# Two layers of experts behind a scan: the blocks of empty rows move from ScalarE's queue to SyncE's

## The chip, the cores and the metric

One core of a Trainium2 chip runs the kernel. The metric is the device time of one execution in microseconds (us); the kernel before has a median of 1076.63 us in 3 runs (1074.83 to 1076.91).

## What is computed

A gated scan over 2 sequences of 5056 tokens with 256 channels gives 10112 rows. Two layers of 8 experts follow; in both, each row goes to one expert (the largest logit) and comes out weighted with that expert's gate:

```python
f = lower_bound + (1 - lower_bound) * sigmoid(f_logit)
h = f[:, t] * h + (1 - f[:, t]) * x[:, t]        # y[:, t] = h
for e in range(8):                               # layer 1, then layer 2 on its output
    mask = expert_idx == e
    out[mask] = gate_w[mask, None] * (relu(x[mask] @ w1[e]) @ w2[e])   # 256 -> 1024 -> 256
```

Layer 1 finds its logits from normalised rows and normalised expert vectors divided by tau, layer 2 from `x @ w_gate`.

## The kernel before

Rows are sorted by expert through a table in DRAM, one per layer (X[0], X[1]; the trace shows both as X). Each expert has a region of its own in it, large enough for all rows. A row is written to its expert's next free place by an indirect DMA of GpSimd (p_put for layer 1, m_slot for layer 2), as two fp16 halves of its 256 values, its gate and its number.

The matmuls work on tiles of 128 rows of one expert. A tile is loaded by SyncE with a transposing DMA (t_load: xT<-X), its gates and row numbers with a small one (exr<-X); four buffers hold such tiles (XB). The hidden width of 1024 is done in two halves, and a **unit** is one tile and one half: 24 matmuls into hps (mm1, L827), an eviction by ScalarE (hT, L835) whose remainder VectorE takes (L188), and three units later 12 matmuls (mm2, L849). For layer 1's output ScalarE, VectorE and GpSimd then make the row for layer 2 (squares L872, scaled halves L887, logits, rank, place); for layer 2's output ScalarE scales it and GpSimd writes it out.

Which tile belongs to which expert is known only at run time. So now and then a **plan** is made (checkpoint): from the counters of rows per expert (RK) VectorE works out a table of expert and first row for the next tiles (tab), and the engines read its entries into registers. Layer 1 has four plans after 16, 32, 48 and 64 groups of 128 rows and a last one after all of them, layer 2 has one after 65 and a last one. Up to the last plan only full tiles are used. Behind the last plan each expert's region ends in a tile that is only partly filled; to make that safe, one block of 128 empty rows (zrow, 258 words of 4 bytes each, 132 KB a block) is written behind each expert's last row. That is pad_rows: `pads` holds, per expert, the place of the first free row, the engine loads the eight numbers into registers (L705) and issues one DMA per expert (L708). In the kernel before ScalarE does this, one block in each of the eight units behind the plan (`padn` is 1):

```python
for e in range(E):
    at(now[0] + 1 + e // cfg["padn"], 13, pad_rows, m, pads, e)
```

The order is written out by hand: `at(unit, priority, function)` puts each piece of work into a unit, and from unit 17 on the queues of TensorE, SyncE, GpSimd and ScalarE keep that order; VectorE's is chosen by a scheduler. Weights of layer 2 are loaded (ws, 512 KB, from ScalarE's queue), split into fp16 halves (W, ScalarE L397 and VectorE L188) and come in units between the others.

Dependencies through X are declared by hand. Row writes carry group Xw, blocks Xp, reads Xr. x_write frees a write from waits for Xw and Xr; a row write is freed from Xp too, a block is not, so each block waits for the block before it. x_read keeps the first `xcnt[key]` writes as dependencies of a tile's load; for a tile of the last plan these are all row writes and the eight blocks. do_loads puts loads up to six units ahead into SyncE's order, and stops at a tile whose writes have not all been put into the program yet.

Of the kernel before, what the change touches and what calls it, by code (L numbers as in the profile page):

```python
# [17 lines left out]
P = 128  # L18
D = 256
E = 8  # L20
# [97 lines left out]
 't0at': (-3, 40),  # L118
 'w1at': (16766, 49534),
 'w2at': (82048, 114816),  # L120
 'padn': 1,
 'xq': 'S'}


# [1 line left out]
def scan_moe_moe_kernel(ctx, tc, xf, emb, cst, tmp, w1a, w2a, w1b, w2b, out, seq, cfg=CFG):  # L126
# [5 lines left out]
    DUM = E * CAP  # L132
# [45 lines left out]
    X = [dr.tile([DUM + P, RW // 2], I32, name=f"X{m}") for m in range(2)]  # L178
# [5 lines left out]
    V, A, G, T, SP = nc.vector, nc.scalar, nc.gpsimd, nc.tensor, nc.sync  # L184

    def stt(eng, out, in0, s, in1, op0, op1, **kw):
        assert eng is V
        return eng.scalar_tensor_tensor(out=out, in0=in0, scalar=s, in1=in1, op0=op0, op1=op1, **kw)  # L188

    def ts(eng, out, in0, s1, s2, op0, op1=None):  # L190
        if op1 is None:
            return eng.tensor_scalar(out=out, in0=in0, scalar1=s1, scalar2=None, op0=op0)  # L192
        return eng.tensor_scalar(out=out, in0=in0, scalar1=s1, scalar2=s2, op0=op0, op1=op1)  # L193

    def tt(eng, out, in0, in1, op):
        return eng.tensor_tensor(out=out, in0=in0, in1=in1, op=op)  # L196

    xw = [[], []]  # L200
    pval = {}

    def ins_of(i):
        return getattr(i, "ins", i)

    def x_write(m, i, group="Xw"):
        i = ins_of(i)
        tc.declare_no_dep(i, group=f"Xw{m}", reason="disjoint rows")
        tc.declare_no_dep(i, group=f"Xr{m}", reason="disjoint rows")
        if group == "Xw" and pval:  # L210
            tc.declare_no_dep(i, group=f"Xp{m}", reason="disjoint rows")
        tc.add_to_no_dep_group(f"{group}{m}", i)
        xw[m].append(i)

    def x_read(m, i, key):
        i = ins_of(i)
        assert len(xw[m]) >= xcnt[key]
        keep = xw[m][:xcnt[key]]
        tc.declare_no_dep(i, group=f"Xw{m}", keep=keep, reason="ordered by hand")
        if (m, E - 1) in pval:  # L220
            tc.declare_no_dep(i, group=f"Xp{m}", keep=keep, reason="ordered by hand")
        tc.add_to_no_dep_group(f"Xr{m}", i)
        for w in keep:
            tc.add_manual_dep(i, w.name, mybir.DependencyInfo(mybir.DependencyClass.Sync, mybir.DependencyReason.DATA),
                              reason="rows of the tile table")
# [55 lines left out]
    zrow = [None]  # L281
# [59 lines left out]
    def setup_c(em, tau_t, trf, wgf):  # L341
        z = zero_rows()
        for m in range(2):
            x_write(m, G.dma_start(out=X[m][DUM:DUM + P, :], in_=z))
        V.memset(ones16, 1.0)
        V.memset(c64, 64.0)
        s0 = sm.tile([P, G4 + CT, E], F16, name="s0", tag="s0", bufs=1)
        for e in range(E):
            V.memset(s0[:, :, e:e + 1], float(CAPT * e))
        yield  # L350
        T.matmul(out=RK, lhsT=ones16, rhs=s0, start=True, stop=True, skip_group_check=True)
        V.tensor_copy(out=tri16, in_=trf)
        yield
        ts(V, tri16b, tri16, -1.0, 1.0, ALU.mult, ALU.add)
        yield
        V.tensor_copy(out=id16, in_=idt)
        yield
        ts(V, idn, idt, -1.0 / 64.0, None, ALU.mult)
        yield
        for m in range(2):  # L360
            G.memset(pt[m], 0.0)
        yield
        ts(V, wgh, wgf, 64.0, None, ALU.mult)
        yield
        stt(V, wgl, wgf, 64.0, wgh, ALU.mult, ALU.subtract)


    now = [0]
# [316 lines left out]
    def p_put(q, rows):  # L685
        p = pq[q]
        for i in rows:
            if i >= p["g"]:
                return
            x_write(0, G.indirect_dma_start(out=X[0], out_offset=IndirectOffsetOnAxis(ap=p["sl"][:, i, 0:1], axis=0),  # L690
                                            in_=p["row"][:, i, :].bitcast(I32), in_offset=None, bounds_check=BOUND,
                                            oob_is_err=False))
            yield
# [4 lines left out]
    nums = {}  # L698
    counted = [0, 0]

    preg = [A.alloc_register(f"pa{i}") for i in range(E)]

    def pad_rows(m, pads, e):
        if e == 0:
            A.load(preg, pads[0:1, 0:E])  # L705
            for i in range(E):
                pval[m, i] = A.snap(preg[i], donate=True, min_val=0, max_val=DUM)
        x_write(m, A.dma_start(out=X[m][ds(pval[m, e], P), :], in_=zrow[0]), "Xp")  # L708

    def checkpoint(m, n, final, key, done):  # L710
        c8 = RK[:, rkb[m][0]:rkb[m][0] + 1, :]
        if final:
            pads = tb.tile([P, E], I32, name="pads", tag=f"pads{m}")
            ts(V, pads, c8[:, 0, :], pid, None, ALU.add)
            for e in range(E):
                at(now[0] + 1 + e // cfg["padn"], 13, pad_rows, m, pads, e)
        xcnt[key] = 1 + done + (E if final else 0)
        assert counted[m] == done
        ct = tb.tile([P, 6, E], F32, name="ct", tag="ct")
        ci = tb.tile([P, E], I32, name="ci", tag="ci")  # L720
        stt(V, ci, c8[:, 0, :], float(P - 1 if final else 0), ebase, ALU.add, ALU.subtract)
        ts(V, ci, ci, 7, None, ALU.arith_shift_right)
        av, q, ex, v, w, tk = (ct[:, i] for i in range(6))
        V.tensor_copy(out=v, in_=ci)
        tt(V, av, v, pt[m], ALU.subtract)
        V.tensor_tensor_scan(out=q, data0=av, data1=av, initial=0.0, op0=ALU.add, op1=ALU.bypass)
        tt(V, ex, q, av, ALU.subtract)
        tt(V, v, pt[m], ex, ALU.subtract)
        stt(V, v, v, float(P), ebase, ALU.mult, ALU.add)
        tt(V, w[:, 0:E - 1], v[:, 1:E], v[:, 0:E - 1], ALU.subtract)  # L730
        ts(V, w[:, E - 1:E], v[:, E - 1:E], -1.0, float(DUM), ALU.mult, ALU.add)
        tab = tb.tile([P, 2, n], I32, name="tab", tag=f"tab{key}" if final or n > 4 else f"tab4_{int(key) % 8}")
        step = -(-n // -(-n // (D // (E + 1))))
        for j0 in range(0, n, step):
            k = min(step, n - j0)
            lew = op.tile([P, D], F32, name="le", tag="ob")
            le = lew[:, 0:k * E].rearrange("p (n e) -> p n e", e=E)
            ef = lew[:, k * E:k * (E + 1)].unsqueeze(2)
            ei, ri = (tab[:, i, j0:j0 + k] for i in range(2))
            jj = jt[:, j0:j0 + k]  # L740
            tt(V, le, q.unsqueeze(1).to_broadcast([P, k, E]), jj.unsqueeze(2).to_broadcast([P, k, E]), ALU.is_le)
            V.tensor_reduce(out=ef, in_=le, axis=AX.X, op=ALU.add)
            ts(V, ei, ef[:, :, 0], float(E - 1), float(ESTEP), ALU.min, ALU.mult)
            tt(V, le, le, w.unsqueeze(1).to_broadcast([P, k, E]), ALU.mult)
            V.tensor_reduce(out=ef, in_=le, axis=AX.X, op=ALU.add)
            stt(V, ef[:, :, 0], jj, float(P), ef[:, :, 0], ALU.mult, ALU.add)
            i = ts(V, ri, ef[:, :, 0], v[:, 0:1], float(DUM), ALU.add, ALU.min)
        if not final:
            ts(V, tk, ex, -1.0, float(n), ALU.mult, ALU.add)
            ts(V, tk, tk, 0.0, None, ALU.max)  # L750
            tt(V, tk, tk, av, ALU.min)
            tt(V, pt[m], pt[m], tk, ALU.add)
        if not tablast:
            tablast.append(ins_of(i))
        tabs[key] = tuple(tab[:, i] for i in range(2))
        if final:
            num = tb.tile([P, 1], I32, name="num", tag=f"num{m}")
            V.tensor_copy(out=num, in_=q[:, E - 1:E])
            nums[m] = num
# [311 lines left out]
    def at(s, prio, fn, *a):  # L1071
        seqn[0] += 1
        slots.setdefault(s, []).append((prio, seqn[0], fn, a))
# [154 lines left out]
    def cp1():  # L1228
        for m, cnt, n, fin, key in cpl:
            if m == 1 and key not in xcnt and cnt <= routed[0]:  # L1230
                checkpoint(m, n, fin, key, routed[0])
# [84 lines left out]
    with ExitStack() as region:  # L1316
# [5 lines left out]
        i = first - 2  # L1322
# [117 lines left out]
```

## Time and profile before

| | before |
|---|---|
| median of 3 runs | 1076.63 us (1074.83 to 1076.91) |
| profiled execution | 1075.63 us |
| its span, first to last instruction | 1073.8 us |
| TensorE busy | 1003.0 us (93%) |
| VectorE, ScalarE, GpSimd busy | 604.3, 525.3, 432.7 us |
| mean granted TensorE clock | 0.981 |
| bytes moved by DMA | 132.72 MB |

The profile gives, for one execution, the time each engine worked, and for each gap of an engine what ended it (the releaser). PE is TensorE, DVE VectorE, ACT ScalarE, POOL GpSimd, SP SyncE; ACTq and SPq are instructions that only issue a DMA or load registers. A clock of 1.00 is 2.4 GHz, one of 0.50 is 1.2 GHz. Times in us count from the first instruction.

### The profile page before, as it was taken

What the parts mean: (1) busy time and instruction counts of PE and PEld (TensorE: products, weight loads), DVE (VectorE), ACT (ScalarE), POOL (GpSimd) and SP (SyncE); (2) the same over time, 40 slices, a digit from 0 to 9 for tenths busy, and PEclk for the clock granted to TensorE, in tenths of its full rate; (3) what the DMA queues carried; (4) which work ended last, traced back from release to release, by engine and by line L of the source; (5) the groups of instructions that cost most, each with busy time, mean ns of one, the idle gap of its engine ahead of it and who ended that gap; (6) DMA issues with size and microseconds to landing.
All of it is one profiled execution on the core that took longest, in us unless ns stands there. A gap on an engine that the chain in (4) does not pass through costs nothing. (4 is left out here: it accounts for less than half of the span.)

```text
span 1073.8 us, 37047 instructions
## 1 busy us (share of the span) xinstructions
PE 1003.0 (93%) x13267; PEld 933.6 (87%) x13267; DVE 604.3 (56%) x2007; ACT 525.3 (49%) x1301; POOL 432.7 (40%) x864
## 2 busy tenths in 40 slices
PE   4557999999999999889999999899999999999997
PEld 4436889999999998779999998899999999999997
DVE  8989767787778776556429876543222222222221
ACT  6888455655555654456336564543333333333332
POOL 4276756667776665222101551143222222222222
PEclk9967999999999999989999999999999999999999
DMA  9699425876665773555459589843322222222220
GB/s 352 204 331 236 120 68 115 136 142 115 130 134 135 137 120 91 154 156 151 108 113 259 121 173 219 157 100 84 55 55 51 51 51 52 46 52 44 46 51 31
DMA packets 195616, 132.72 MB, mean 124 GB/s; under 512 B 169601, under 2 KB 172558, under 8 KB 195440
## 3 DMA queue, kind: packets, MB, share of 16 engines
q1 hardware_dynamic: 170080, 58.07, 27.5%
q10 hardware_dynamic: 13504, 40.74, 15.3%
q0 software_dynamic: 11856, 31.51, 11.0%
q8 instruction: 118, 1.93, 0.8%
q14 instruction: 58, 0.48, 0.2%
HBM read 58.89 MB, written 38.85 MB: 91 GB/s over the span
## 5 line engine op out<-in xcount | busy, mean ns | idle before, releaser
L827 PE MATMUL hps<-xT,W 128*128 128x128 f16 x7968 | 508.4, 220 | 16.7 <-DVE hT L188 5.8
L827 PEld LDWEIGHTS <-W 128*128 x7968 | 476.5, 98 | 29.5 <-issue 16.3
L849 PE MATMUL ops<-W,hT 128*128 x3984 | 492.5, 273 | 2.8 <-ACT W L397 1.0
L188 DVE SCALAR_TENSOR_TENSOR hT<-hps,hT 128x512 f16<-128x512 f32 x332 | 228.3, 688 | 343.3 <-ACT hT L835 325.9
L849 PEld LDWEIGHTS <-hT 128*128 128x128 f16 x3984 | 375.1, 98 | 44.1 <-issue 4.1
L835 ACT ACTIVATE hT<-hps 128x512 f16<-128x512 f32 x332 | 197.7, 596 | 336.9 <-PE hps L827 258.5
L1017 POOL DMA_INDIRECT out<-osum,ti x83 | 81.3, 979 | 301.2 <-ACT osum L1013 176.6
L995 POOL DMA_INDIRECT X<-trow,tsl x83 | 98.4, 1186 | 49.5 <-DVE tsl L188 16.4
L690 POOL DMA_INDIRECT X<-row,sl x79 | 88.8, 1124 | 69.8 <-issue 25.3
L1013 ACT ACTIVATE osum<-ops,exr 128x256 f32<-128x256 f32 x62 | 29.4, 474 | 47.0 <-PE ops L849 44.8
L196 POOL TENSOR_TENSOR lf<-exr,us 128x2 f32<-128x2 f32 (+1 forms) x42 | 9.5, 226 | 105.2 <-DVE us L192 52.0
L188 DVE SCALAR_TENSOR_TENSOR W<-ws,W 128x1024 f16<-128x1024 f32 x34 | 41.4, 1221 | 7.3 <-ACT W L397 7.2
L531 PE MATMUL yt<-cs,xf 128*128 128x128 f32 x126 | 27.9, 299 | 16.2 <-DVE xf L516 13.6
L516 DVE TENSOR_TENSOR_SCAN xf<-xf 128x256 f32<-128x256 f32 (+3 forms) x64 | 42.7, 708 | 0.1
L397 ACT ACTIVATE W<-ws 128x1024 f16<-128x1024 f32 x35 | 36.9, 1058 | 9.1 <-DMA ws<-w1b 5.0
L872 ACT ACTIVATE trow<-osum 128x256 f16<-128x256 f32 x83 | 35.1, 423 | 12.4 <-DMA X<-trow,tsl 4.9
L861 ACT ACTIVATE osum<-ops 128x256 f32<-128x256 f32 x58 | 22.2, 382 | 35.4 <-PE ops L849 29.0
L188 DVE SCALAR_TENSOR_TENSOR trow<-osum,tsc,trow 128x256 f16<-128x256 f32 x83 | 37.4, 481 | 3.3 <-ACT trow L887 1.7
L533 PEld LDWEIGHTS yt<-cs,xf 128*128 128x128 f32 x252 | 35.3, 204 | 0.8 <-issue 0.7
L188 DVE SCALAR_TENSOR_TENSOR row<-yt,sc,row 128x256 f16<-128x256 f32 x79 | 36.0, 472 | 0.0
L887 ACT ACTIVATE trow<-osum,tsc 128x256 f16<-128x256 f32 x62 | 28.1, 500 | 14.8 <-DVE tsc L193 11.9
L571 ACT ACTIVATE row<-yt,sc 128x256 f16<-128x256 f32 x79 | 33.1, 478 | 3.2 <-DVE sc L193 3.2
(161 smaller groups left out, 956.6 us busy)
## 6 DMA issues: line engine op xcount, KB each, us to landing
xf<-xf ACTq DMA_DIRECT2D x28, 512.0 KB
ws<-w1b ACTq DMA_DIRECT2D x16, 512.0 KB
ws<-w2b ACTq DMA_DIRECT2D x16, 512.0 KB
W<-w1a SPq DMA_DIRECT2D x11, 512.0 KB
W<-xf SPq DMA_DIRECT2D x8, 512.0 KB
ws<-w2a ACTq DMA_DIRECT2D x8, 512.0 KB
WD<-wq SPq DMA_DIRECT2D x8, 512.0 KB
W<-WD SPq DMA_DIRECT2D x8, 512.0 KB
```

Of the source, the lines that this page charges most:

```text
L188: return eng.scalar_tensor_tensor(out=out, in0=in0, scalar=s, in1=in1, op0=op0, op1=op1, **kw)
L397: A.activation(out=hi, in_=src, func=ACTF.Copy, scale=64.0)
L516: V.tensor_tensor_scan(out=t[:, k, lo:hi], data0=t[:, 2 + k, lo:hi], data1=t[:, k, lo:hi], initial=init, op0=ALU.mult, op1=ALU.subtract)
L533: T.matmul(out=yt[:, D:D + E], lhsT=t[:, k, i * P:(i + 1) * P], rhs=ide[:, (1 - k) * (P + E):(1 - k) * (P + E) + E], start=(k == 0), stop= ...
L571: A.activation(out=p["row"][:, o + i, 0:D], in_=yv(d["yt"][i]), func=ACTF.Copy, scale=p["sc"][:, o + i:o + i + 1])
L690: x_write(0, G.indirect_dma_start(out=X[0], out_offset=IndirectOffsetOnAxis(ap=p["sl"][:, i, 0:1], axis=0), in_=p["row"][:, i, :].bitcast( ...
L827: T.matmul(out=hps[:, c, :], lhsT=w, rhs=xt[:, a, :], start=(n == 0), stop=(n == 5))
L835: A.activation(out=hh[:, 0], in_=hps, func=ACTF.Relu)
L849: T.matmul(out=o, lhsT=hT[:, a + k, :], rhs=w[:, b * D:(b + 1) * D], start=(first and k == 0 and n == 0), stop=(last and k == 3 and n == 2))
L872: A.activation(out=d["row"][:, i, D:2 * D], in_=t["O"], func=ACTF.Square, scale=0.25, accum_out=d["ss"][:, i:i + 1])
L995: x_write(1, G.indirect_dma_start(out=X[1], out_offset=IndirectOffsetOnAxis(ap=sl[:, i, 0:1], axis=0), in_=d["row"][:, i].bitcast(I32), in ...
L1017: i = ins_of(G.indirect_dma_start(out=out, out_offset=IndirectOffsetOnAxis(ap=ti, axis=0), in_=r, in_offset=None, bounds_check=N - 1, oob_ ...
```

## The change

SyncE takes the place of ScalarE in pad_rows. The eight blocks of a layer are issued in one run, in the first unit behind the plan with priority 0, ahead of that unit's tile loads (do_loads has priority 1). And a block is freed from waits for other blocks: x_write declares no dependency on group Xp as soon as a block of the layer exists.

```diff
     xw = [[], []]
+    xpad = [[], []]
     pval = {}
...
-        if group == "Xw" and pval:
+        if xpad[m]:
             tc.declare_no_dep(i, group=f"Xp{m}", reason="disjoint rows")
         tc.add_to_no_dep_group(f"{group}{m}", i)
         xw[m].append(i)
+        if group == "Xp":
+            xpad[m].append(i)
...
-    preg = [A.alloc_register(f"pa{i}") for i in range(E)]
-
-    def pad_rows(m, pads, e):
-        if e == 0:
-            A.load(preg, pads[0:1, 0:E])
-            for i in range(E):
-                pval[m, i] = A.snap(preg[i], donate=True, min_val=0, max_val=DUM)
-        x_write(m, A.dma_start(out=X[m][ds(pval[m, e], P), :], in_=zrow[0]), "Xp")
+    preg = [SP.alloc_register(f"pa{i}") for i in range(E)]
+
+    pnil = SP.alloc_register("pnil")
+
+    def pad_rows(m, pads):
+        SP.load(preg, pads[0:1, 0:E])
+        for e in range(E):
+            SP.reg_mov(pnil, e)
+            pval[m, e] = SP.snap(preg[e], donate=True, min_val=0, max_val=DUM)
+            x_write(m, SP.dma_start(out=X[m][ds(pval[m, e], P), :], in_=zrow[0]), "Xp")
+        SP.reg_mov(pnil, E)
...
-            for e in range(E):
-                at(now[0] + 1 + e // cfg["padn"], 13, pad_rows, m, pads, e)
+            at(now[0] + 1, 0, pad_rows, m, pads)
```

In the order of instructions this looks as follows. The names in square brackets are what an instruction waits for: DMAHW0 to DMAHW7 are the completion counters that all DMAs of SyncE's and ScalarE's queues share in turn, DMASW those of GpSimd's, the others the engines. ISA rows are register work.

ScalarE behind layer 1's last plan, before: the eight blocks lie between evictions, squares and weight loads (two of the eight are shown), and the second one waits for a second counter, that of the block before it.

```order
L861 ACTIVATE osum<-ops 128x256 [waits PE_49]
L705 TENSOR_LOAD pads [waits DVE_49]
L708 ISA
L708 DMA X_99<-zrow 128x258 [waits DMAHW4_49]
L835 ACTIVATE hT<-hps 128x512 [waits PE_49]
...
L384 DMA ws<-w1b 128x1024
L708 ISA
L708 DMA X_99<-zrow 128x258 [waits DMAHW4_49,DMAHW0_49]
L872 ACTIVATE trow,tss<-osum 128x256 [waits DMASW5_49,DMASW4_49,Activation_49]
```

The same place now:

```order
L865 ACTIVATE osum<-ops 128x256 [waits PE_49]
L839 ACTIVATE hT<-hps 128x512 [waits PE_49]
...
L386 DMA ws<-w1b 128x1024 [waits DMAHW2_49]
L876 ACTIVATE trow,tss<-osum 128x256 [waits DMASW5_49,DMASW4_49,Activation_49]
```

The register load and the blocks are gone from ScalarE, and nothing else has changed its place there.

SyncE behind layer 1's last plan, before: two loads of tiles of the plan before, and then the first tile of the last plan, whose load waits for twelve counters.

```order
L802 DMA_TRANSPOSE xT<-X_99 128x4x128 [waits DMAHW2_49,PE_49]
L809 ISA
L809 DMA exr<-X_99 128x2 [waits DMAHW3_49]
L802 ISA
L802 DMA_TRANSPOSE xT<-X_99 128x4x128 [waits DMAHW5_49,PE_49]
L809 ISA
L809 DMA exr<-X_99 128x2 [waits DMAHW6_49,Pool_49]
L791 TENSOR_LOAD tab [waits DVE_49]
L802 ISA
L802 DMA_TRANSPOSE xT<-X_99 128x4x128 [waits DMAHW1_49,DMAHW2_49,DMAHW0_49,DMAHW3_49,DMASW7_49,DMAHW4_49,DMASW6_49,DMAHW6_49,DMASW3_49,DMAHW7_49,DMASW2_49,PE_49]
```

The same place now (six of the eight blocks left out):

```order
L708 TENSOR_LOAD pads [waits DVE_49]
L712 ISA
L712 DMA X_99<-zrow 128x258 [waits DMAHW2_49]
...
L712 DMA X_99<-zrow 128x258 [waits DMAHW1_49]
L806 ISA
L806 DMA_TRANSPOSE xT<-X_99 128x4x128 [waits DMAHW3_49,PE_49]
...
L806 DMA_TRANSPOSE xT<-X_99 128x4x128 [waits DMAHW5_49,PE_49]
...
L795 TENSOR_LOAD tab [waits DVE_49]
L806 ISA
L806 DMA_TRANSPOSE xT<-X_99 128x4x128 [waits DMAHW0_49,DMASW7_49,DMAHW1_49,DMASW6_49,DMAHW2_49,DMASW3_49,DMAHW7_49,DMASW2_49,PE_49]
```

The register load and eight blocks stand ahead of the two loads of the older plan; each block waits for one counter.

SyncE behind layer 2's last plan, now:

```order
L806 DMA_TRANSPOSE xT<-X_100 128x4x128 [waits DMAHW7_49,DMAHW0_49,PE_49]
L708 TENSOR_LOAD pads [waits DVE_49]
L712 ISA
L712 DMA X_100<-zrow 128x258 [waits DMAHW1_49]
...
L712 DMA X_100<-zrow 128x258 [waits DMAHW7_49]
L712 ISA
L712 DMA X_100<-zrow 128x258 [waits DMAHW0_49]
L712 ISA
L712 DMA X_100<-zrow 128x258 [waits DMAHW1_49]
L806 ISA
L806 DMA_TRANSPOSE xT<-X_100 128x4x128 [waits DMAHW3_49,PE_49]
```

Here the first load shown is layer 2's 17th and the last one its 18th; before, the 18th followed the 17th directly. The eighth block waits for the counter that the first block waited for.

## Rows read from the trace of the kernel before

**Rows 1.** Busy by stage: us, engines' busy us, PE clock, DMA share, GB/s

```profile
430.00:470.00 40.00, 32.13 (x409) 28.84 (x407) 18.67 (x71) 17.71 (x43) 10.29 (x20) 0.91 0.52 148
470.00:560.00 90.00, 89.63 (x1261) 84.92 (x1260) 46.11 (x147) 43.77 (x97) 14.65 (x32) 1.00 0.53 127
655.00:690.00 35.00, 29.44 (x387) 26.99 (x385) 19.36 (x31) 17.44 (x31) 0.18 (x1) 1.00 1.07 195
690.00:800.00 110.00, 110.00 (x1502) 104.39 (x1500) 37.91 (x63) 39.78 (x72) 36.49 (x62) 1.00 0.36 74
```

**Rows 2.** Instructions on pads and zrow: ns min/median/max, first and last start

```profile
L192 DVE TENSOR_SCALAR pads<-RK,cs x2: 226/226/226, 425.4 to 649.3; 128x8 int32<-128x8 f32 x2
L705 ACTq TENSOR_LOAD <-pads x2: 542/641/740, 426.4 to 655.9; - x2
...
L708 ACTq DMA_DIRECT2D X<-zrow x16: 338/338/391, 427.3 to 684.1; - x16
```

**Rows 3.** Waits of ScalarE, 425 to 460 us: total us, times, longest

```profile
ACT hT L835 <- DMA X<-zrow: 6.1, 3, 2.8
...
ACT trow L872 <- DMA X<-zrow: 3.4, 2, 2.3
```

**Rows 4.** Waits of SyncE's queue, 420 to 470 us

```profile
SPq L802 <- DMA X<-zrow: 24.1, 1, 24.1
```

**Rows 5.** Timeline of SyncE, layer 1: start, us, instruction

```profile
427.70 1.19 SPq L802 DMA_TRANSPOSE xT<-X  x1
...
458.39 1.21 SPq L802 DMA_TRANSPOSE xT<-X  x1
```

**Rows 6.** Waits of ScalarE, 645 to 690 us

```profile
ACT hT L835 <- DMA X<-zrow: 11.0, 6, 3.2
```

**Rows 7.** Groups of TensorE, 418 to 500 us: busy, mean ns | idle before, releasers

```profile
L915 PE MATMUL x2p<-id,trow 128*128 128x128 f16 x48 | 4.3, 220 | 2.7 <-ACT trow L887 1.5 <-DVE toh L188 0.6 <-PEq L1294 0.3
```

**Rows 8.** Timeline of TensorE, layer 1; in brackets idle time before, releaser

```profile
449.75 1.50 PE L827 MATMUL hps<-xT,W 128*128 128x128 f16 x24
...
452.40 1.50 PE L827 MATMUL hps<-xT,W 128*128 128x128 f16 x24
...
461.65 2.72 PE L827 MATMUL hps<-xT,W 128*128 128x128 f16 x24 [3.99 <-DMA xT<-X]
464.16 2.76 PE L849 MATMUL ops<-W,hT 128*128 x12
466.72 1.83 PE L827 MATMUL hps<-xT,W 128*128 128x128 f16 x24
...
471.29 1.47 PE L849 MATMUL ops<-W,hT 128*128 x12
```

**Rows 9.** Timeline of TensorE, layer 2

```profile
657.46 1.50 PE L827 MATMUL hps<-xT,W 128*128 128x128 f16 x24 [0.45 <-DMA xT<-X]
...
663.18 1.50 PE L827 MATMUL hps<-xT,W 128*128 128x128 f16 x24
...
669.98 1.50 PE L827 MATMUL hps<-xT,W 128*128 128x128 f16 x24 [1.34 <-DVE hT L188]
...
680.00 1.50 PE L827 MATMUL hps<-xT,W 128*128 128x128 f16 x24 [1.91 <-DVE hT L188]
...
683.40 1.50 PE L827 MATMUL hps<-xT,W 128*128 128x128 f16 x24 [0.59 <-DVE hT L188]
...
688.56 1.51 PE L849 MATMUL ops<-W,hT 128*128 x12 [1.01 <-ACT W L397]
```

**Rows 10.** Timeline of SyncE, layer 2

```profile
649.29 1.19 SPq L802 DMA_TRANSPOSE xT<-X  x1
...
653.42 1.19 SPq L802 DMA_TRANSPOSE xT<-X  x1
```

**Rows 11.** Timeline of ScalarE, layer 2

```profile
652.57 0.35 ACTq L384 DMA_DIRECT2D ws<-w2b  x1
...
659.78 1.06 ACT L397 ACTIVATE W<-ws 128x1024 f16<-128x1024 f32 x1 [2.15 <-DMA ws<-w2b]
```

More of the change, by code (lines that the diff above doesn't have):

```diff
@@ L120 @@
  'w2at': (82048, 114816),
- 'padn': 1,
  'xq': 'S'}
```

## The prediction

> **What bounds the kernel now.** I read the busy table by stage first. From 690 us on TensorE is busy for all of its 110 us, and between the two plans, in 470 to 560 us, for 89.63 of 90: it is the engine that sets the time. The reader is to look at the two stages in which it isn't full: in 430 to 470 us it is busy for 32.13 of 40 us at a mean granted clock of 0.91, and in 655 to 690 us for 29.44 of 35 us at full clock [rows 1]. These are the stretches behind the two plans: the first of ScalarE's blocks of empty rows is issued at 427.3 us, the last one at 684.1 us, eight per layer [rows 2]. Since TensorE is full behind each stretch, a microsecond won there should reach the end, and I count it one to one.
>
> Second, the waits. In the first stretch ScalarE waits 6.1 us ahead of evictions (hT) and 3.4 us ahead of squares (trow) for blocks to land [rows 3]. Squares and evictions themselves need nothing of the blocks; they only stand behind one on ScalarE's queue, and each block waits for the one before it. SyncE waits 24.1 us, in one piece, for the same blocks [rows 4]: between its load at 427.70 and the next one at 458.39 us [rows 5] it stands, because the first tile of the last plan may be read only when all eight blocks have landed, and ScalarE lets them out one per unit. In the second stretch ScalarE's evictions wait 11.0 us for blocks [rows 6].
>
> Third, what of this TensorE feels. First layer: 1.5 us ahead of a transposition for rows that ScalarE made late, and 0.6 us for a mask (toh) that VectorE makes from ScalarE's squares [rows 7]; then 3.99 us until the first tile of the last plan (xT) is there. Behind that gap the engine runs at the lower of its two clocks, 1.2 instead of 2.4 GHz, for three groups: 2.72 us where the same 24 matmuls take 1.50, 2.76 where the 12 take 1.47, and 1.83 for 1.50 [rows 8]. Second layer [rows 9]: 1.34, 1.91 and 0.59 us for hT, which VectorE could finish only after ScalarE's late eviction, and 1.01 us for a weight half (W) that ScalarE had still to copy.
>
> **The change, first layer.** Gaps of 0.6 + 1.5 + 3.99 = 6.09 us, and (2.72 - 1.50) + (2.76 - 1.47) + (1.83 - 1.50) = 2.84 us of slow clock: **8.93 us**, of which I take all as gone. What comes in its place on SyncE: it reads the counts two loads earlier in its order than its long wait, ahead of the load at 427.70 us and the one before that. VectorE wrote the counts at 425.4 us in 0.23 [rows 2], so SyncE stands until about 425.7 us, reads registers for 0.64 and issues eight DMAs of 0.34 us [rows 2]; with register work I allow 0.4 to 0.55 us each, 3.2 to 4.4 us, and it is through at 429.5 to 431 us. Queued behind are the two loads of the old plan. The tile loaded at 427.70 us is the last before the gap and feeds the groups of 449.75 and 452.40 us, its forerunner's two groups lie some 5 us before those [rows 5, 8]. The load whose landing the first layer shows took from 458.39 to 461.65 us, 3.26 us [rows 5, 8]; even at 8.17 us (the slowest seen, below) one issued at 431 us is there by 439, and needed near 444. So the block run is covered by about five microseconds; without that cover it would cost what the load is late. The first tile of the last plan can then be asked for as soon as a buffer is free, in the middle of the 430s, 20 us before its use. Next late after the 3.99 us is thus nothing on SyncE, and ScalarE and VectorE are busy for 17.71 and 18.67 of these 40 us [rows 1].
>
> **The change, second layer.** Gone are 1.34 + 1.91 + 0.59 = 3.84 us for hT and, with ScalarE no longer behind, the 1.01 us for the weights: **4.85 us**. But here SyncE has little cover. Each unit, about 2.65 us (449.75 to 452.40), takes a new tile, with four buffers, and the load that started at 649.29 us was waited for until 657.46, 8.17 us [rows 8 to 10]: transfers are slow there, beside weights of 512 KB, one of which, issued at 652.57 us, held ScalarE's copy up until 659.78 [rows 11]. The eight blocks now stand ahead of the load that started at 653.42 us [rows 10]. 0.64 for the registers and 3.2 to 4.4 for the blocks put it at 657.3 to 658.5 us. The seventh block also waits for a completion counter that may be that of the weights landing near 659.8 us; with that, the load starts near 660.9. Its tile was needed at 663.18 us, two groups after the one at 657.46 [rows 9]. Landing 3.26 us after its start, it is late by nothing to 1.0 us; at 8.17 us by up to 5.9, and a pause of that size may bring the slow clock, 2.84 us by the first layer's rows. Lower bound 0: an earlier load of another tile is no gain while TensorE is full. Upper bound 5.9 + 2.84 = 8.7 us. I take **2.0 us**: 1.0 by the quiet price, and about 1 more because the blocks on the queue ahead, 8 x 132 KB = 1.06 MB, need 5.4 us at this stage's 195 GB/s [rows 1], a little longer than their issue lasts.
>
> **What else moves.** ScalarE sheds 16 issues of 0.34 and two register loads of 0.64 us, 6.7 us in all [rows 2]; it is idle for half of both stretches, so I give that nothing. The same 16 transfers run, crowded into two bursts; near the first nothing is in need of the queue, the second is in the 2.0 us.
>
> The sum: -8.93 - 4.85 + 2.0 = **-11.78 us** against the profiled execution's 1075.63 us, 1063.85 us; the median is 1.0 us above that execution, so **1064.9 us**.
>
> **A rule against the change.** ScalarE lost 6.1 + 3.4 + 11.0 = 20.5 us to waits for the blocks and 16 x 0.34 = 5.4 us to issuing them [rows 2, 3, 6]. The Trainium skill, DMA: Bandwidth & Descriptors, section Issuing engines are not separate DMA queues, says that DMAs started from several engines run on the same 16 DMA engines and interleave, and that another issuing engine saves only the time to initiate them, usually small beside the transfer. By that alone the change would be worth about nothing (rival c); the rows speak against it, since most of the loss is order and waiting on the issuing queue.
>
> **The rivals.**
>
> (a) The burst only moves the loss to the tile loads of the second layer. For: the load of 8.17 us, and the 0.45 us that TensorE already waited for it [rows 9, 10]. Against: a block is a quarter of one weight load. It costs 8.7 instead of 2.0 us: -8.93 - 4.85 + 8.7 = -5.1, so 1071.5 us.
>
> (b) Slower: the eight blocks still land one after the other, now on SyncE, and hold up every tile load of the second layer. In the first layer they took from 427.3 until SyncE was released near 458.4 us, 31 us or 3.9 each; at that price the load of 653.42 us would start at 685 and land at 688, 25 us late: -13.78 + 25 = +11, so 1088 us. It decides the sign from a blockade of some 20 us on (13.8 us won and the 6 us that are covered), 2.5 us per block. Against: in the new order a block waits for one counter each, not for the block before; only the last may share its counter with the first.
>
> (c) Nothing changes: only issue time moves, ScalarE's waits lie beside other work, and the first tile of the last plan is held by the rows' other writers until then anyway. For: TensorE's gaps are small beside ScalarE's waits. Against: SyncE's one wait names the blocks. Price: at best the small gaps, up to 2 us, so 1074.6 to 1076.6 us.
>
> **How the numbers follow.** The forecast gets 0.69 (1061 to 1068 us), (a) 0.22, (b) 0.04, (c) 0.05. For the range I take the forecast and (a): downwards no loss in the second layer (1062.9) and, since nobody's wait explains 1.5 us of what 430 to 470 us still lacks (40 - 32.13 - 6.09 = 1.8), these gone too, 1061, rounded to 1060.5; upwards (a), rounded to 1072. About 0.2%, 2.2 us, is what a measurement of this kernel can tell from no change. Faster by more: 0.69 + 0.22 = 0.91; within: (c), 0.05; slower: (b), 0.04.
>
> **What would show it.** First layer: no wait of ScalarE for X<-zrow, SyncE's first load of the last plan near 435 instead of 458 us, no gap of several microseconds and clock 1.00 in 430 to 470 us. If ScalarE still keeps TensorE waiting there, my 2.1 us of small gaps are wrong; if SyncE does, the 6.83 us of gap and slow clock. Second layer: TensorE's gaps ahead of its groups now put down to xT, not to hT; their sum against my 2.0 us decides between the forecast and (a). If SyncE's own waits show block after block, it is (b). I am wrong altogether if both stretches gain and the same time comes back as gaps of TensorE between 470 and 640 us or behind 690 us.

## The result and the profile after

The changed kernel has a median of 1064.08 us in 10 runs (1062.0 to 1072.43), the kernel before 1075.81 us in 10 runs on the same chip (1071.8 to 1082.44). The ratio is 0.9902, with a 95% interval of 0.9873 to 0.9932: 10.5 us less, 7.3 to 13.7. Forecast was 1064.9 us. On a second chip the ratio was 0.9934 (0.9905 to 0.9962), 7.1 us. All ratios here are formed from single runs and not from the medians, and leave out three runs in a slower state (two of "layer 2 alone" and one of before, below), which medians and ranges count. So the sign was right; whether the mechanism and the terms were is the question of the experiments.

The profiled execution of after took 1063.67 us (span 1061.8, mean granted clock 0.984), 11.96 us less than that of before. Its stages, in the form of [rows 1]; the last two rows are as long as the stretches of before that begin when VectorE writes the counts and end at 470 and 690 us:

```profile
430.00:470.00 40.00, 39.48 (x572) 37.13 (x570) 26.30 (x91) 25.03 (x60) 13.04 (x28) 1.00 0.80 188
470.00:560.00 90.00, 88.81 (x1226) 83.49 (x1224) 45.17 (x133) 41.88 (x91) 11.52 (x24) 1.00 0.64 135
640.00:655.00 15.00, 9.58 (x126) 8.88 (x124) 8.99 (x20) 6.43 (x11) 0.00 (x0) 0.99 1.09 263
690.00:800.00 110.00, 110.00 (x1493) 104.30 (x1491) 35.66 (x58) 38.94 (x71) 34.07 (x58) 1.00 0.35 69
423.00:467.60 44.60, 44.08 (x638) 41.49 (x637) 30.81 (x121) 26.61 (x63) 16.40 (x29) 1.00 0.80 191
635.50:676.20 40.70, 35.04 (x459) 33.05 (x458) 24.27 (x50) 21.62 (x37) 1.65 (x2) 0.96 0.93 198
```

The same two stretches of before:

```profile
425.40:470.00 44.60, 36.73 (x476) 33.22 (x474) 23.11 (x98) 19.28 (x46) 13.78 (x25) 0.92 0.52 145
649.30:690.00 40.70, 35.14 (x465) 32.41 (x464) 24.94 (x51) 22.21 (x38) 1.08 (x2) 1.00 1.08 208
```

Behind the first plan TensorE is busy for 44.08 of 44.60 us instead of 36.73, at full clock. Behind the second it is busy for no longer than before (35.04 against 35.14 us), and at 0.96 instead of 1.00: in this pair of executions the second layer won nothing. The instructions on the counts and the blocks, against [rows 2], say the same by their times:

```profile
L191 DVE TENSOR_SCALAR pads<-RK,cs x2: 211/216/220, 423.0 to 635.5; 128x8 int32<-128x8 f32 x2
L708 SPq TENSOR_LOAD <-pads x2: 527/529/531, 423.3 to 639.0; - x2
...
L712 SPq DMA_DIRECT2D X<-zrow x16: 332/332/1227, 424.0 to 646.2; - x16
```

The first plan stands 2.4 us earlier (423.0 instead of 425.4), the second 13.8 us (635.5 instead of 649.3), the end 12.0. Ahead of the first plan both kernels run the same program, so its 2.4 us are not the change's. It brought 11.4 us between the plans, and behind the second it lost 1.8.

SyncE behind the first plan, against [rows 5] (start, us, instruction), and its one wait for blocks, against 24.1 us in [rows 4]:

```profile
423.99 4.53 SPq L712 DMA_DIRECT2D X<-zrow  x8
428.71 1.61 SPq L806 DMA_TRANSPOSE xT<-X  x1
...
431.14 1.20 SPq L806 DMA_TRANSPOSE xT<-X  x1
...
436.43 1.21 SPq L806 DMA_TRANSPOSE xT<-X  x1
```

```profile
SPq L806 <- DMA X<-zrow: 0.3, 1, 0.3
```

The eight blocks take 4.53 us, the two loads of the older plan follow at once, and the first tile of the last plan is asked for at 436.43 instead of 458.39 us. ScalarE's waits of [rows 3] have shrunk to one of 2.9 us (trow), which TensorE doesn't feel: between 418 and 475 us its only two gaps above 0.3 us are those below, against 3.99 us and three groups at the lower clock in [rows 8].

```profile
460.31 0.61 PE L919 MATMUL x2p<-id,trow 128*128 128x128 f16 x8 [0.52 <-DVE tse L981]
472.77 0.61 PE L919 MATMUL x2p<-id,trow 128*128 128x128 f16 x8 [0.95 <-PEq L1298]
```

SyncE and TensorE behind the second plan, against [rows 9, 10]:

```profile
639.68 6.81 SPq L712 DMA_DIRECT2D X<-zrow  x8
646.72 12.76 SPq L806 DMA_TRANSPOSE xT<-X  x5
```

```profile
655.24 2.72 PE L831 MATMUL hps<-xT,W 128*128 128x128 f16 x24 [5.66 <-DMA xT<-X]
657.75 1.69 PE L853 MATMUL ops<-W,hT 128*128 x12
```

The gaps for hT and W of [rows 9] are gone, and ScalarE waits for no block any more. In their place stands one gap for a tile. The run of blocks lasts 6.81 us; the load behind it begins at 646.72 us, its tile was needed at 655.24 - 5.66 = 649.58 and came at 655.24, 8.5 us after the issue. A load of the quiet price would have been 0.4 us late. Behind the gap TensorE again runs at the lower clock for a group and part of a second.

### The profile page after: what moved, and what is told of

It reads as the page before. It is cut to its first block, busy times and chain, and to the rows that moved or that the text cites. A ratio compares the mean times of both kernels' runs of the same rounds, so it can differ in the third digit from the quotient of the medians.

```text
span 1061.8 us, 37047 instructions
## 1 busy us (share of the span) xinstructions
PE 996.5 (94%) x13267; PEld 932.1 (88%) x13267; DVE 603.8 (57%) x2007; ACT 529.3 (50%) x1301; POOL 431.7 (41%) x864
## 5 line engine op out<-in xcount | busy, mean ns | idle before, releaser
L533 PE MATMUL yt<-cs,xf 128*128 128x128 f32 x126 | 28.2, 300 | 16.7 <-DVE xf L518 13.8
L891 ACT ACTIVATE trow<-osum,tsc 128x256 f16<-128x256 f32 x62 | 28.1, 500 | 16.0 <-DVE tsc L192 11.4
L187 DVE SCALAR_TENSOR_TENSOR xf<-xf 128x512 f32<-128x512 f32 (+1 forms) x32 | 21.8, 682 | 23.2 <-POOL xf L192 19.4
```

## The experiments

The theory: what was won is the order (all blocks early) and the blocks' independence of one another; in the second layer the run holds up tile loads, as the prediction's 2.0 us say. Its rivals: only ScalarE's queue matters; the blocks are bound to land one after another; or the loss of the second layer is larger than priced and can be avoided. All kernels but the repeat of after set per layer the engine, the first unit behind the plan, the units per block (0: all in one run) and the priority, in one table in place of after's fixed call. Of after the table would be:

```python
pads_at = (('SP', 1, 0, 0), ('SP', 1, 0, 0))    # layer 1, layer 2
```

and of before `('A', 1, 1, 13)` twice, chained, though the table's pad_rows then differs from before's in one dependency, told under "One layer at a time". `chained` below stands for the pair in x_write that says of which layer the blocks wait for each other:

```python
if xpad[m] and not (group == "Xp" and chained[m]):
```

The times, each beside before on the same chip:

| kernel | median, us (lowest to highest, runs) | ratio to before (95%) | us against before |
|---|---|---|---|
| after again | 1064.22 (1060.23 to 1067.6, 8) | 0.9934 (0.9905 to 0.9962) | -7.1 |
| layer 1 alone* | 1066.39 (1063.27 to 1071.02, 12) | 0.9957 (0.9935 to 0.998) | -4.6 |
| layer 2 alone* | 1072.35 (1060.16 to 1080.11, 12) | 0.9986 (0.9949 to 1.0024) | -1.5 |
| layer 2's run late | 1057.22 (1053.58 to 1059.41, 6) | 0.9864 (0.983 to 0.9897) | -14.6 |
| independent, spread on ScalarE* | 1068.69 (1064.78 to 1075.53, 10) | 0.9986 (0.9955 to 1.0017) | -1.5 |
| one run on ScalarE | 1060.39 (1056.13 to 1061.76, 4) | 0.9897 (0.9857 to 0.9937) | -11.0 |
| one run on SyncE, chained | 1086.21 (1084.89 to 1088.06, 4) | 1.0154 (1.0119 to 1.019) | +16.5 |
| layer 2 spread on SyncE* | 1072.31 (1069.7 to 1077.7, 10) | 1.0017 (0.999 to 1.0044) | +1.8 |
| the same, loads freed | 1064.3 (1060.41 to 1066.8, 4) | 0.9876 (0.9836 to 0.9916) | -13.4 |
| spread on ScalarE, loads freed | 1071.99 (1066.43 to 1080.01, 10) | 0.9951 (0.9916 to 0.9986) | -5.3 |
| layer 1's run on ScalarE, layer 2's late | 1062.12 (1060.73 to 1066.8, 4) | 0.9863 (0.9827 to 0.99) | -14.8 |

The kernel before had medians of 1072.35 us (rows 1 to 4), 1070.98 (5 to 8) and 1078.05 (9 to 11); the last column is the ratio's share of these. In the kernels with a star blocks and tile loads alternate in a layer, and these loads wait for blocks.

**One layer at a time.**

```diff
-pads_at = (('SP', 1, 0, 0), ('SP', 1, 0, 0))
+pads_at = (('SP', 1, 0, 0), ('A', 1, 1, 13))     # chained in layer 2
```

> Only the first layer's blocks are issued by SyncE in one run and declared independent; the second layer's stay on ScalarE, one per unit, each waiting for the one before. The prediction's terms: first layer -8.9 us, second layer nothing, so about 1067 us where the kernel before has 1075.8. The profile of the changed kernel suggests more: between the two plans it gained 11.4 us (VectorE's counts of the second layer come 13.8 us earlier, those of the first 2.4 us), and it lost 1.8 us behind the second plan. By that this kernel gains 9 to 11 us, its second stretch looks like that of the kernel before (ScalarE waits 8 to 11 us for blocks, TensorE 3 to 5 us for hT), and it is within 2 us of the changed kernel. A rival, that most of the gain belongs to the second layer (ScalarE's waits are longest there), gives -4 us or less.

```diff
-pads_at = (('SP', 1, 0, 0), ('SP', 1, 0, 0))
+pads_at = (('A', 1, 1, 13), ('SP', 1, 0, 0))     # chained in layer 1
```

> Only the second layer's blocks are issued by SyncE in one run; the first layer's stay on ScalarE as before. By the prediction -4.85 + 2.0 = -2.9 us against the kernel before. By the profile of the changed kernel, in which TensorE stood 5.66 us for a tile behind the second plan and ran 1.5 us longer at the slow clock, the 4.85 us won are paid back with 7.1: between +1 and +3 us, so no gain at all, with one gap of 4 to 7 us ahead of a group that waits for xT. If the gap is below 3 us, the profiled execution of the changed kernel was an unlucky one and the prediction's 2.0 us stands.

Layer 1 alone brought 4.6 us (2.1 to 7.0), layer 2 alone 1.5 (2.6 slower to 5.5 faster), beside the 7.1 of both; of the first 9 to 11 us were expected. But in neither kernel is the other layer as it was before. The kernel before enters all eight places of a layer into `pval` with the first block; the table's pad_rows enters each with its own block. And x_read frees a tile load of the older plan from the blocks already issued only `if (m, E - 1) in pval`: in before from the first block on, with the table from the eighth on. As long as blocks and loads alternate, those loads now wait for blocks that they don't touch. SyncE's waits for blocks behind the second plan, of before and then of layer 1 alone (632 to 700 us; in all, times, longest), and TensorE's largest gap there in the latter:

```profile
SPq L809 <- DMA X<-zrow: 1.4, 1, 1.4
```

```profile
SPq L816 <- DMA X<-zrow: 19.8, 7, 7.4
```

```profile
658.01 2.72 PE L841 MATMUL hps<-xT,W 128*128 128x128 f16 x24 [4.39 <-DMA xT<-X]
```

The same behind the first plan in layer 2 alone, against one wait of 24.1 us in [rows 4]:

```profile
SPq L816 <- DMA X<-zrow: 27.1, 2, 17.5
```

So these two kernels don't price the layers of the change. In the first, layer 1's stretch is as full as in after (39.38 of 40 us in 430 to 470 us, at clock 1.00), and its second layer has a gap of 4.39 us for a tile that [rows 9] don't have. What the second does show is the changed layer 2 once more, with a gap of nearly the size of after's 5.66 us, as expected:

```profile
660.49 2.38 PE L841 MATMUL hps<-xT,W 128*128 128x128 f16 x24 [4.88 <-DMA xT<-X]
```

**After again, and the second run late.** Unit 60 behind the plan lies where loads have more room.

```diff
-pads_at = (('SP', 1, 0, 0), ('SP', 1, 0, 0))
+pads_at = (('SP', 1, 0, 0), ('SP', 60, 0, 0))
```

> The changed kernel once more, beside the others on the same chip. Both theories: about 1064 us, 10 to 13 us below the kernel before. The profile tells whether the gap of 5.66 us for xT behind the second plan repeats (the theory that the run of blocks holds up the loads: 4 to 7 us again) or was an accident of that execution (prediction: about 2 us).

> As the changed kernel, but the second layer's run of blocks is issued 60 units (about 160 us) behind its plan instead of one; their tiles are used some 90 units behind it. If the blocks in front of the tile loads cause the gap behind the second plan, it goes, and with it the slow clock: 7 us less than the changed kernel by its profile, 2 us less by the prediction's term, so 1057 or 1062 us, with no gap over 1 us of TensorE in that stretch and none where the blocks now stand (transfers are sparse there, a tile has four buffers in hand). If the gap stays, the loads are late for the weights' sake alone and moving the blocks changes nothing.

Late is faster than after by 0.7% (0.9864 against 0.9934, intervals apart): about 7.5 us (no run of either falls into the range of the other), the size that the profile of after had suggested, and beats both kernels. TensorE behind the second plan, first of the repeat of after (640 to 700 us), then of the late run:

```profile
652.39 1.50 PE L831 MATMUL hps<-xT,W 128*128 128x128 f16 x24 [2.17 <-DVE hT L187]
669.21 1.50 PE L831 MATMUL hps<-xT,W 128*128 128x128 f16 x24 [0.72 <-DMA xT<-X]
```

```profile
646.54 1.50 PE L841 MATMUL hps<-xT,W 128*128 128x128 f16 x24 [0.47 <-DMA xT<-X]
667.13 1.50 PE L841 MATMUL hps<-xT,W 128*128 128x128 f16 x24 [1.88 <-DMA xT<-X]
```

and the stretch in which the late run's eight blocks stand (the last one at 798.0 us):

```profile
700.00:800.00 100.00, 100.00 (x1360) 94.84 (x1358) 30.42 (x48) 34.25 (x63) 28.16 (x48) 1.00 0.36 73
```

The repeat of after shows 2.89 us of gaps at full clock, of which only 0.72 are for a tile, where the first execution had 5.66 and slow clock and layer 2 alone 4.88; so what the run costs in its place changes from one execution of the same order to the next. The late run still has a gap of 1.88 us for a tile, where none over 1 us was expected. The two profiles differ by 2.1 us in their spans (1058.5 and 1056.4) and can't show 7.5; that number is the timed runs' alone. Moved to a stretch with a DMA share of 0.36, the blocks cost TensorE nothing.

**Engine, order or independence.** Three kernels take the change's three parts apart: independent blocks in the old places on ScalarE; one run of independent blocks on ScalarE; after with the chain back.

```diff
-pads_at = (('SP', 1, 0, 0), ('SP', 1, 0, 0))
+pads_at = (('A', 1, 1, 13), ('A', 1, 1, 13))     # independent
```

> Blocks stay on ScalarE, one per unit, but are declared independent of one another: the second half of the change alone. If the chain of blocks is what costs, ScalarE's waits for X<-zrow fall from some 20 us to under 4, the small gaps of the first layer (2 us) and the gaps for hT in the second (4 us) go: -6 us against the kernel before. If the unit-by-unit issue costs, the first layer's gap for the first tile of the last plan stays, 2 to 4 us with the slow clock behind it, because SyncE's load still has to follow the eighth block, eight units behind the plan. I expect both: 3 to 7 us below the kernel before, 4 to 6 above the changed one.

```diff
-pads_at = (('SP', 1, 0, 0), ('SP', 1, 0, 0))
+pads_at = (('A', 1, 0, 13), ('A', 1, 0, 13))     # independent
```

> One run of independent blocks right behind each plan, but on ScalarE's queue, in its place there (priority 13), so that SyncE's tile loads are not behind them on the queue. If order and independence bring the gain and not the engine, the first layer is as in the changed kernel (no gap over 1 us, SyncE's first load of the last plan near 435 us) but for 1 to 2 us that ScalarE is late by the eight issues (8 x 0.34 us and their waits). In the second layer the same megabyte moves at the same time on another queue: if the loads were late in the changed kernel because they stand behind the blocks on SyncE's queue, the gap for xT there falls below 3 us; if it is the crowd of transfers, it stays at 3 to 7 us. In all within 4 us of the changed kernel.

```diff
-if xpad[m]:
+if xpad[m] and not (group == "Xp" and (True, True)[m]):
```

> The changed kernel, but each block waits for the one before it, as it did on ScalarE: rival (b) of the prediction, built. Eight blocks at 2 to 4 us each hold SyncE's tile loads for 16 to 30 us behind each plan. The first layer covers about 13 us from the end of the run (its next tiles are needed near 444 us): a gap of 3 to 15 us there; in the second layer a gap of 8 to 22 us, in both with the slow clock behind it. So 10 to 35 us above the changed kernel, above the kernel before. If it stays below that kernel, an undisturbed block lands in less than 2 us and the price that the rival put on it, 3.9 us, came from ScalarE's other work between the blocks.

One run on ScalarE is as good as after: 0.9897. Its first stretch and its run, on ScalarE's timeline:

```profile
430.00:470.00 40.00, 40.00 (x584) 37.99 (x582) 28.29 (x96) 27.57 (x66) 13.47 (x28) 1.00 0.74 190
```

```profile
424.43 4.61 ACTq L716 DMA_DIRECT2D X<-zrow  x8
429.08 0.60 ACT L849 ACTIVATE hT<-hps 128x512 f16<-128x512 f32 x1 [5.24 <-DVE toh L187]
```

TensorE is busy for all 40 us although ScalarE spends 4.61 us on the run. So the words "by SyncE" in the change carry nothing; here the rule of the Trainium skill that the prediction set against the change (DMA: Bandwidth & Descriptors, section Issuing engines are not separate DMA queues) holds: which engine issues is worth nothing that these runs can measure (0.9897 against 0.9902 and 0.9934, each with some 0.3 to 0.4% either way). What the rule doesn't speak of is what the queue waits for, and there the time lies. Behind the second plan the same kernel has these gaps:

```profile
644.96 1.50 PE L841 MATMUL hps<-xT,W 128*128 128x128 f16 x24 [1.26 <-DMA xT<-X]
648.48 1.50 PE L841 MATMUL hps<-xT,W 128*128 128x128 f16 x24 [0.71 <-DMA xT<-X]
653.78 1.50 PE L841 MATMUL hps<-xT,W 128*128 128x128 f16 x24 [2.49 <-DVE hT L187]
```

The gaps for tiles are below 3 us, which by the expectation speaks for the place on SyncE's queue as the cause in after; but the repeat of after had only 0.72. Whether the queue or the crowd of transfers makes the loads late stays open.

Independent blocks in the old order brought 1.5 us (1.8 slower to 4.8 faster), less than expected. But this kernel, too, has the added waits of the older plan's loads: 22.4 us in two pieces behind the first plan, where before has one of 24.1. With those loads freed, as they are in before, independence alone is worth 5.3 us (1.5 to 9.1; "spread on ScalarE, loads freed", below). In both the first tile of the last plan still comes late, by 3.75 and 3.69 us, since the eighth block still leaves ScalarE eight units behind the plan. The new order with the chain left in makes the kernel slower than before by 16.5 us. SyncE's waits and TensorE's gap, first and second layer:

```profile
SPq L716 <- DMA X<-zrow: 19.0, 7, 4.3
```

```profile
449.99 2.72 PE L841 MATMUL hps<-xT,W 128*128 128x128 f16 x24 [12.22 <-DMA xT<-X]
```

```profile
SPq L716 <- DMA X<-zrow: 16.7, 7, 4.2
```

```profile
675.94 2.72 PE L841 MATMUL hps<-xT,W 128*128 128x128 f16 x24 [14.68 <-DMA xT<-X]
```

Seven waits of 2.7 and 2.4 us in the mean: that is rival (b) as it was described. The run without independence loses; independence without the run wins a part, and the gap of 3.69 us that it leaves ahead of the last plan's first tile is what the run takes away in layer 1.

**The spread blocks of layer 2, and the loads' waits for them.** If the crowd of the run costs in layer 2, the blocks could be spread there, one per unit, on SyncE:

```diff
-pads_at = (('SP', 1, 0, 0), ('SP', 1, 0, 0))
+pads_at = (('SP', 1, 0, 0), ('SP', 1, 1, 13))    # independent
```

> As the changed kernel, but the second layer's blocks are issued by SyncE one per unit, independent, each behind its unit's tile load, in the eight units behind the plan. If the run of eight in front of one load is what makes it late, 1 block of 0.4 us per unit is covered and the second layer's gaps come down to those without blocks, 2 to 4 us in all: 3 us below the changed kernel, 3 above the one with the late run. If the extra megabyte in this crowded stretch costs, whatever its order, it is no better than the changed kernel.

The whole gain is gone (1.0017), although layer 1's stretch is as full as in after (39.22 of 40 us in 430 to 470 us): against the expectation, the second layer lost about what the first had won. SyncE's waits and timeline, 632 to 700 us:

```profile
SPq L816 <- DMA X<-zrow: 17.9, 7, 4.4
```

```profile
644.35 0.34 SPq L716 DMA_DIRECT2D X<-zrow  x1
648.78 1.19 SPq L816 DMA_TRANSPOSE xT<-X  x1
650.16 0.43 SPq L716 DMA_DIRECT2D X<-zrow  x1
655.19 1.19 SPq L816 DMA_TRANSPOSE xT<-X  x1
```

Each of seven tile loads behind a block waits for that block, 2.6 us in the mean, though it reads full tiles of the older plan that no block touches. The reason is the condition in x_read told above: as long as blocks and loads alternate, each load waits for every block put in before it; in one run, all loads behind it are free. The wait is the experiments' own: neither before, whose condition holds from the first block on, nor after, with its run, has it. To test it, the loads are freed from the first block on, in the spread kernel and in the one with independent blocks on ScalarE:

```diff
-        if (m, E - 1) in pval:
+        if xpad[m]:
             tc.declare_no_dep(i, group=f"Xp{m}", keep=keep, reason="ordered by hand")
```

> The spread blocks of layer 2 once more (SyncE, one per unit, independent), but tile loads of the older plan that stand between the blocks no longer wait for the blocks already issued. Theory A, the spread kernel lost its gain because each of those loads waits until the block ahead of it has landed (17.9 us of SyncE's waits in 7 pieces): with that wait gone the second layer costs no more than with the run, 1057 to 1065 us, about 8 to 12 us under the spread kernel's 1072, and SyncE's waits between 640 and 690 us name X<-zrow for under 5 us in all. Theory B, it is the place of the blocks between the loads or the shared completion counters that costs: 1069 to 1074 us as before, and the waits for X<-zrow stay.

> Blocks from ScalarE, one per unit, independent of each other, and loads of the older plan freed from blocks already issued. Theory A (the loads' waits for blocks cost the second layer about 4 to 6 us, the late eighth block costs the first layer 4 to 8 us by the first tile of the last plan): 1063 to 1067 us, second stretch without an xT gap over 2 us, first stretch with its gap of 2 to 4 us ahead of the first tile of the last plan and one SyncE wait for X<-zrow over 8 us. Theory B, only blocks in one run bring anything: 1068 to 1072 us, with an xT gap of 3 us or more in the second stretch too.

On SyncE the one line is worth 1.4% (0.9876 against 1.0017, intervals apart). Its timeline of SyncE and its stretch, to be read against 644.35 and following above and against 29.44 of 35 us in [rows 1]:

```profile
652.75 0.34 SPq L716 DMA_DIRECT2D X<-zrow  x1
653.45 2.29 SPq L815 DMA_TRANSPOSE xT<-X  x1
655.93 0.43 SPq L716 DMA_DIRECT2D X<-zrow  x1
656.56 1.20 SPq L815 DMA_TRANSPOSE xT<-X  x1
```

```profile
655.00:690.00 35.00, 35.00 (x482) 33.20 (x479) 20.59 (x28) 20.16 (x35) 3.70 (x7) 1.00 0.84 191
```

No wait of SyncE for X<-zrow is left there, and TensorE is full. The blocks of layer 2 need not come in one run, then, once loads don't wait for them. That spread blocks beat the run isn't shown: the ratio is below after's 0.9902 and 0.9934, but the intervals overlap. On ScalarE the line took the ratio from 0.9986 to 0.9951 (intervals overlap), and the two stretches show gaps that are left there. SyncE's wait and TensorE's gaps, layer 1, then layer 2:

```profile
SPq L816 <- DMA X<-zrow: 21.0, 1, 21.0
```

```profile
459.59 2.40 PE L841 MATMUL hps<-xT,W 128*128 128x128 f16 x24 [3.69 <-DMA xT<-X]
...
664.74 2.72 PE L841 MATMUL hps<-xT,W 128*128 128x128 f16 x24 [2.12 <-DMA xT<-X]
...
686.04 2.72 PE L841 MATMUL hps<-xT,W 128*128 128x128 f16 x24 [3.54 <-DMA xT<-X]
```

In time it is 5.3 us below before; the median of 1071.99 us lies in theory B's range, but before is 6 to 7 us slower on this chip than on the two of the other experiments, and the ratio speaks for A. The profiled execution took 1078.31 us, the second longest of ten, so its gaps are not the usual ones. In layer 1 the last plan's first tile waits for the eighth block, as expected. In layer 2 I had expected no gap over 2 us, and there are two; SyncE waits there for weights (4.9 us in one piece) and for earlier tiles (7.8 us in three), not for blocks. Before has such waits as well (for weights 4.5 us in three pieces, for tiles 3.1 in one); why they are larger here than with the blocks on SyncE stays open.

**Both best places.** Last, the run of layer 1 on ScalarE with the late run of layer 2:

```diff
-pads_at = (('SP', 1, 0, 0), ('SP', 1, 0, 0))
+pads_at = (('A', 1, 0, 13), ('SP', 60, 0, 0))
```

> First layer's run of independent blocks from ScalarE, second layer's run from SyncE 60 units behind its plan. If what decides is when the blocks stand and that they are independent, not the engine, this is as fast as the changed kernel with the late second run: 1054 to 1060 us, TensorE busy for over 39 of 40 us in 430 to 470 us and without a gap over 2 us in 640 to 700 us. If SyncE matters in the first layer, 2 us or more slower than that, 1060 to 1064 us, with gaps for hT or rows of ScalarE between 430 and 470 us.

The ratio of 0.9863 is that of the late run with SyncE in both layers (0.9864), on another chip where before, too, was about 6 us slower (1078.05 against 1072.35); so the median of 1062.12 fell in the range of the rival theory, while the ratio speaks for the first. By that ratio, known to some 0.4%, the engine makes no difference in layer 1. TensorE's 37.80 of 40 us (not over 39, as expected) hold one pause of 1.25 us at 434.99 that names no releaser but "issue".

## Why the prediction was right, and where its steps were off

**The mechanism of layer 1: right.** SyncE's first load of the last plan at 436.43 us ("near 435"), the block run through at 423.99 + 4.53 = 428.5 us (429.5 to 431 was worked out, with counts 2.4 us later), no gap of several microseconds, clock 1.00: the signs that were named came, but for one wait of ScalarE of 2.9 us that TensorE doesn't feel. But the prediction let ScalarE's share of the loss, the move off its queue, pass as part of the cause; with the run on ScalarE the gain is the same. What wins is that the blocks stand early and don't wait for one another.

**The two gains: about the right size.** The late run has layer 1 as in after and no blocks among layer 2's loads behind the plan, so it shows both gains without the loss, as far as the moved blocks cost nothing: 14.6 us (11.0 to 18.2), where -8.93 - 4.85 = -13.78 was worked out. How this divides between the layers isn't timed, since the kernels with one layer alone change the other layer too. In the profiled pair the first stretch gave 44.08 - 36.73 = 7.35 us of gaps and 2.84 of slow clock, 10.2, more than the term of 8.93. The 1.8 us of that stretch which no wait explained hold a pause put down to "issue", 1.5 us in 423 to 447 us of before:

```profile
L827 PE MATMUL hps<-xT,W 128*128 128x128 f16 x171 | 11.2, 219 | 1.5 <-issue 1.5
```

Such pauses of 1 to 3 us stand elsewhere in other executions, of the changed kernels too, so this part was not the change's to take.

**The loss of layer 2: too small.** 2.0 us were taken between bounds of 0 and 8.7; by the late run it is 7.5 us in timed runs. The profiles of three executions show what it consists of and how it varies: 5.66 us of gap and (2.72 - 1.50) + (1.69 - 1.47) us of slow clock, 7.1 in all, in the first; a gap of 4.88 us in layer 2 alone; 0.72 us for a tile in the repeat. The step that failed is the choice of the quiet price, 3.26 us for the load behind the run, with 1 us more for the blocks' bytes: in the first execution that load took 8.5 us, the "8.17 us by up to 5.9" that was kept as the far end. The run itself, 6.81 us with the waits for counters, was sized at 3.2 to 4.4; that alone made the load 2.4 to 3.6 us later.

**The sum.** -11.78 us lies in the interval of the first chip (7.3 to 13.7 us less) and outside that of the second (4.1 to 10.2). On the second chip, where gains and loss were taken apart, the loss eats 7.5 of the 14.6 us. That 1064.9 stands 0.8 us from the median of the first is thus partly luck: by the second chip the loss was taken 5.5 us too small, and the profiled pair's 11.96 us hold 2.4 from ahead of the change. The 0.2% that the prediction took as what a measurement can tell was too little: the intervals are 0.3% wide to either side.

**The rivals.** (a), a loss of up to 8.7 us in layer 2, is nearer to the measured size than the forecast's 2.0. Its sum of -5.1 us lies in the interval of the second chip, where the forecast doesn't, and outside that of the first, where the forecast does. (b) is refuted for after and confirmed as a mechanism: with the chain back the kernel is 16.5 us slower than before, where +11 was worked out. That is near for a wrong reason in part: a block costs 2.6 to 2.9 us in the chain instead of 3.9, but layer 1, for which (b) charged nothing, stands 12.22 us too. Its eight blocks hold SyncE for 23.1 us in layer 1 and 20.8 in layer 2, both past the 20 us from which it should decide the sign. (c) is refuted, as the gain is not "issue time", though its premise about the engine holds.

## What to carry to other kernels

When a queue in order waits for something, ask of each instruction behind it what it waits for by name, reads included: in the spread kernel a condition that frees reads too late cost the whole gain. And a kernel that is to put the old form back has to put its dependencies back too: three of the experiments don't, and can't be read as parts of the change. Where a transfer may stand anywhere, put it where the engines and the DMA have room, not where its data is ready. And read a stall's size from several executions before adding it to a sum; one trace tells the mechanism, not the price.

## What the runs showed of the chip that I had not expected

- A tile load took 3.3 us in the first layer [rows 5, 8] and 8.5 us behind the run of blocks and beside weights of 512 KB, in stretches with a DMA share of 0.52 [rows 1] and 1.09 (640 to 655 us of after): a factor of 2.6 for the same 128 rows.
- Eight independent block DMAs left a queue in 4.53 us (SyncE) or 4.61 us (ScalarE) behind the first plan, and in 6.81 us behind the second, where SyncE waited 2.0 us of it for tile loads under way; in a chain on SyncE seven of them needed 20.22 us.
- Executions of one kernel on one chip spread by 1% (before: 1071.8 to 1082.44 us; after: 1062.0 to 1072.43). A gap for the same tile load can be part of it: behind the second plan of after, 5.66 us in one execution, at most 0.72 in another of the same kernel on a second chip.
